# Linear attention block on one core: phi of q on pairs of PSUM banks, one normalising instruction per block of rows, and a changed order of denominators and state accumulator

## The chip, the cores and the metric

The kernel runs on one core of a Trainium2 chip. The metric is the device time of one execution in microseconds. A run is an execution with its own time and with a record of the TensorE clock that was granted, as a share of full speed. Most quoted times are medians of 4 to 11 executions on the same chip, the kernel's executions with executions of the kernel before interleaved in the same rounds. Faster or slower needs a difference of 2%; inside it, an interval of the ratio that leaves out 1 still shows a difference. An execution counts as slow, and is left out, when it takes over 1.5% longer than the fastest of the same kernel; the others are called fast. The sets of rounds ran on different chips, so a comparison between sets carries about 0.1 us of doubt. The span that the profile shows is about 1.7 us shorter than the device time.

Engines: PE is TensorE's matmul stream, PEld its weight loads, DVE is VectorE, ACT is ScalarE, POOL is GpSimd, SP the queue that issues most DMAs.

## The reference, cut to what matters

```python
B, S, D = 1, 2048, 640; H = 32; Dh = 20
q, k, v = split_heads(x @ wqkv)                       # cut: reshape and transpose
phi = lambda t: where(t > 0, t + 1, exp(t)) + 1e-6
pq, pk = phi(q), phi(k)
kv  = einsum("bhsd,bhse->bhde", pk, v)
z   = einsum("bhsd->bhd", pk)
num = einsum("bhqd,bhde->bhqe", pq, kv)
den = einsum("bhqd,bhd->bhq", pq, z)[..., None] + 1e-6
out = merge_heads(num / den) @ wo                     # cut: transpose and reshape
```

The kernel computes phi as min(exp(t), 1) + 1e-6 + max(t, 0), and 1/den as exp(-ln(den)).

## The kernel before

Its stages are: 16 k tiles (matmul, exp on ScalarE, two instructions on VectorE); two passes of state matmuls over the 16 row tiles (`p_step`), with the sum z of phi(k) on VectorE beside them (`z_steps`); the small per-head products (`kv_group`, `w2_group`), which go through HBM to change their layout (`w2_rows`, arriving as `w2p`); the q stage, 20 tiles of 128 columns by 512 rows; four denominators (`den`) and four normalisings; 16 output tiles. Every engine gets a list of instructions, in the order of the calls below; the trace after the change shows VectorE keeping to it (zc read at 64.58 us, though its input was complete at 62.89). Waits on semaphores are derived from the tiles and banks that each instruction reads and writes. The program divides PSUM, the memory that the matmuls write, into 8 banks of 512 columns; it makes a matmul into a bank wait until the bank's last reader is done.

```python
def p_step(h, st):
    def mm(e):
        for d in range(NC_):                     # 5 accumulators, banks 0 to 4
            r = e.matmul(bank(d, HALF), xn[...], pk[...], start=(st == 0), stop=(st == NT - 1))
        return r
    P.add("pe", mm, reads=[("xn", st // 4), ("pk", st)], writes=[("bank", d) for d in range(NC_)])

def q_tile(sbk, c, b):
    ...                                          # 5 matmuls of 128x512 into bank b
    P.add("act", lambda e: e.activation(t[:, :], bank(b), ACTF.Exp), ...)
    P.add("dve", lambda e: e.tensor_scalar(t[:, :], t[:, :], 1.0, 1e-6, ALU.min, ALU.add), ...)
    P.add("dve", lambda e: e.scalar_tensor_tensor(pq[...], bank(b), 0.0, t[:, :], ALU.max, ALU.add), ...)

def z_finish(b):                                 # 5 products with a single column (shown by the profile as 10 fp32 matmuls)
    ...
    P.add("dve", lambda e: e.tensor_copy(zc[:, 0:NC_], bank(b, NC_)), ...)
    for c in range(NC_):
        P.add("dve", lambda e, c=c: e.tensor_scalar(zb[...], hm[:, :], zc[:, c:c + 1], None, ALU.mult), ...)

def den(sbk, b):
    ...                                          # 5 matmuls zb x pq into bank b; needs all of zb
    P.add("act", lambda e: e.activation(lb[i][:, :], bank(b), ACTF.Ln, bias=eps[:, 0:1]), ...)
    P.add("act", lambda e: e.activation(rd[i][:, :], lb[i][:, :], ACTF.Exp, scale=-1.0), ...)

def normalize(sbk):
    for c in range(NC_):
        P.add("dve", lambda e, v=v: e.tensor_tensor(v, v, rd[i][:, :], ALU.mult), ...)

# after the state passes (cut: the calls before and after)
kv_group(0)
next_q(5)
z_finish(4)
w2_group(0, 2)
next_q(6)
w2_group(1, 0)
den(0, 4)
next_q(7)
...
```

## Time and profile before

| | |
|---|---|
| median (range) | 111.82 us (111.79 to 111.96), 4 executions, granted clock 1.00 in the profiled one |
| span of the profile | 110.1 us |
| PE busy | 101.5 us, 92% |
| DVE, ACT busy | 66.9 us, 41.9 us |

The page's second part cuts the span into 40 slices of 2.75 us; each digit is the busy share in tenths (9 is 90% or more), and PEclk is the granted clock in tenths.

```profile
PE   5969999999799999999999999993999799999990
...
PEclk9999999999999999999999999999999999999999
```

PE is close to full from the first k tile to the end, with one hole in the q stage (the 3) and a few smaller ones. The same matmuls run before and after the change (662 recorded on each of the two pages). The view of waits names the larger holes; its columns are the waiting engine and line, what it waited for, total us, times, longest us:

```profile
...
PE ps L275 <- DVE pq L288: 1.8, 1, 1.8
...
PE ps L249 <- DVE pk L240: 0.7, 1, 0.7
...
```

The second line is the first state step, which waits for bank 4 to be read by the last phi of k but one. The timeline of PE where the q stage begins (start, length of the run, line, count):

```profile
60.21 1.25 PE L275 MATMUL ps<-xT,wqp 128*128 128x512 bf16 x5
61.30 1.17 PE L325 MATMUL ps<-ones,zs 128*128 128x1 f32 x10
62.33 0.46 PE L365 MATMUL ps<-wog,kvt 120*120 120x320 bf16 x2
62.85 1.02 PE L275 MATMUL ps<-xT,wqp 128*128 128x512 bf16 x4
63.71 0.44 PE L365 MATMUL ps<-wog,kvt 120*120 120x320 bf16 x2
64.21 1.25 PE L391 MATMUL ps<-pq,zb 128*128 128x512 bf16 x5
```

Between z_finish (L325) and the first denominator (L391) stand a q tile and two w2 groups. They cover most of the time in which VectorE makes zb. (Of the q tile one matmul's record is missing.) The groups of instructions that the change replaces, with total busy us and the mean ns of one:

```profile
...
L283 ACT ACTIVATE eq<-ps 128x512 bf16<-128x512 f32 x20 | 11.9, 595 | 21.2 <-PE ps L275 20.7
...
L288 DVE SCALAR_TENSOR_TENSOR pq<-ps,eq 128x512 bf16<-128x512 f32 x20 | 13.8, 692 | 0.7
L285 DVE TENSOR_SCALAR eq<-eq 128x512 bf16<-128x512 bf16 x20 | 5.8, 290 | 12.8 <-ACT eq L283 12.6
...
L407 DVE TENSOR_TENSOR pq<-pq,rd 128x512 bf16<-128x512 bf16 x20 | 7.0, 417 | 2.0 <-ACT rd L400 2.0
```

### The profile page before, as it was taken

The numbers are of one execution on the slowest core, as the hardware profiler recorded it, in microseconds if no ns is written. First come the engines' busy times: TensorE is split into PE (matmuls) and PEld (weight loads), VectorE is DVE, ScalarE is ACT, GpSimd is POOL, SyncE is SP. The second block draws the span as 40 slices with busy tenths as digits, with TensorE's granted clock in tenths as the row PEclk, the third lists the DMA queues.
The fourth block names the chain that finished last, engine by engine and source line by source line (L and its number), as shares of the span: only waits on it lengthen the run. The fifth ranks groups of instructions, "written<-read, shape, count | busy, mean of one in ns | idle before, by whom it ended". The sixth has DMA issues, their size and how long they took to land.

```text
span 110.1 us, 1693 instructions
## 1 busy us (share of the span) xinstructions
PE 101.5 (92%) x662; PEld 64.0 (58%) x668; DVE 66.9 (61%) x132; ACT 41.9 (38%) x73; POOL 5.9 (5%) x16
## 2 busy tenths in 40 slices
PE   5969999999799999999999999993999799999990
PEld 2327777777477674676757745431446377777760
DVE  1004888998899899701137664969849837333331
ACT  3104555555500206202043379872575173333330
POOL 7100000750000000000000000000000000000000
PEclk9999999999999999999999999999999999999999
DMA  1999999999980000000000000082720032433333
GB/s 40 270 295 220 224 211 298 378 363 364 258 163 22 0 0 3 0 0 0 6 0 3 0 0 0 18 216 70 206 92 0 0 119 92 152 119 119 119 120 118
DMA packets 19497, 12.88 MB, mean 117 GB/s; under 512 B 10914, under 2 KB 19490, under 8 KB 19490
## 3 DMA queue, kind: packets, MB, share of 16 engines
q1 hardware_dynamic: 18178, 11.96, 39.4%
q10 hardware_dynamic: 1312, 0.82, 2.7%
q8 instruction: 5, 0.08, 0.3%
q14 instruction: 2, 0.02, 0.0%
HBM read 6.72 MB, written 3.44 MB: 92 GB/s over the span
## 4 chain that ended last, share of the span: by engine, by line
PE 70%; DVE 15%; DMA 6%; ACT 5%; issue 1%
PE ps L225 19%; PE ps L416 17%; PE ps L249 15%; PE ps L275 12%; DMA xT<-in_x_dram 6%; DVE pq L288 4%; PE ps L391 4%; DVE za L294 4%; ACT eq L283 2%; DVE eq L285 2%; DVE pq L407 2%; PE ps L344 1%; ACT lb L398 1%; PE ps L365 1%; ACT rd L400 1%
## 5 line engine op out<-in xcount | busy, mean ns | idle before, releaser
L275 PE MATMUL ps<-xT,wqp 128*128 128x512 bf16 x95 | 23.0, 379 | 2.0 <-DVE pq L288 1.8
L249 PE MATMUL ps<-pk,xn 128*128 128x320 bf16 x160 | 22.4, 299 | 0.8 <-DVE pk L240 0.7
L225 PE MATMUL ps<-wk,xT 128*128 128x320 bf16 x160 | 21.9, 299 | 1.1 <-DMA xT<-in_x_dram 1.1
L416 PE MATMUL ps<-w2p,pq 128*128 128x320 bf16 x160 | 22.2, 299 | 0.3 <-DVE pq L288 0.3
L249 PEld LDWEIGHTS ps<-pk,xn 128*128 128x128 bf16 x160 | 15.5, 98 | 7.9 <-DVE pk L240 1.0
L225 PEld LDWEIGHTS ps<-wk,xT 128*128 128x128 bf16 x160 | 15.6, 98 | 7.5 <-issue 1.5
L283 ACT ACTIVATE eq<-ps 128x512 bf16<-128x512 f32 x20 | 11.9, 595 | 21.2 <-PE ps L275 20.7
L416 PEld LDWEIGHTS ps<-w2p,pq 128*128 128x128 bf16 x160 | 15.6, 98 | 7.0 <-DVE pq L288 0.6
L235 ACT ACTIVATE ek<-ps 128x640 bf16<-128x640 f32 x16 | 11.3, 704 | 15.7 <-PE ps L225 15.7
L275 PEld LDWEIGHTS ps<-xT,wqp 128*128 128x128 bf16 x100 | 9.6, 98 | 12.2 <-DVE pq L288 2.2
L288 DVE SCALAR_TENSOR_TENSOR pq<-ps,eq 128x512 bf16<-128x512 f32 x20 | 13.8, 692 | 0.7
L285 DVE TENSOR_SCALAR eq<-eq 128x512 bf16<-128x512 bf16 x20 | 5.8, 290 | 12.8 <-ACT eq L283 12.6
L240 DVE SCALAR_TENSOR_TENSOR pk<-ps,ek 128x640 bf16<-128x640 f32 x16 | 13.2, 824 | 0.6
L425 DVE CAST osb<-ps 128x320 bf16<-128x320 f32 x16 | 7.7, 489 | 9.6 <-PE ps L416 9.5
L237 DVE TENSOR_SCALAR ek<-ek 128x640 bf16<-128x640 bf16 x16 | 6.1, 380 | 10.5 <-ACT ek L235 10.4
L423 ACT CAST osb<-ps 128x320 bf16<-128x320 f32 x16 | 6.8, 425 | 12.6 <-PE ps L416 12.5
L407 DVE TENSOR_TENSOR pq<-pq,rd 128x512 bf16<-128x512 bf16 x20 | 7.0, 417 | 2.0 <-ACT rd L400 2.0
L216 PE MATMUL ps<-zero 128*128 128x512 bf16 x16 | 5.2, 494 | 1.3 <-DVE eps L147 1.3
L261 ACT CAST pt<-ps 128x320 bf16<-128x320 f32 x6 | 2.2, 434 | 9.7 <-PE ps L249 9.7
L294 DVE TENSOR_TENSOR za<-pk 128x1280 f32<-128x1280 bf16 x4 | 5.7, 1483 | 0.0
L391 PE MATMUL ps<-pq,zb 128*128 128x512 bf16 x19 | 4.8, 380 | 0.4 <-DVE pq L288 0.3
L208 POOL COPY wqp<-wqn 128x640 bf16<-128x640 bf16 x5 | 3.6, 756 | 16.9 <-DMA wqn<-in_wqkv_dram 16.9
(30 smaller groups left out, 36.1 us busy)
## 6 DMA issues: line engine op xcount, KB each, us to landing
xn<-in_x_dram SPq DMA_DIRECT2D x4, 640.0 KB, 9.7
out_dram<-osb SPq DMA_DIRECT2D x16, 160.0 KB, 1.8
wk<-in_wqkv_dram ACTq DMA_DIRECT2D x2, 400.0 KB, 5.0
wqn<-in_wqkv_dram SPq DMA_DIRECT2D x1, 800.0 KB, 5.2
wv<-in_wqkv_dram SPq DMA_DIRECT2D x1, 800.0 KB, 14.3
w2p<-w_rows SPq DMA_DIRECT2D x5, 160.0 KB, 2.7
wog<-in_wo_dram SPq DMA_DIRECT2D x1, 750.0 KB, 14.8
w_rows<-w2g SPq DMA_DIRECT2D x1, 750.0 KB, 5.3
```

Of the source, the lines that this page charges most:

```text
L225: r = e.matmul(bank(b + h, HALF), xT[:, c * S + 128 * st:c * S + 128 * st + 128], wk[:, c * D + HALF * h:c * D + HALF * (h + 1)], start=(c ...
L235: P.add("act", lambda e: e.activation(fold(t[:, :]), two_banks(b), ACTF.Exp), reads=banks + ["table"], writes=[("ek", st % 3)])
L240: P.add("dve", lambda e: e.scalar_tensor_tensor(fold(pk[:, st * D:(st + 1) * D]), two_banks(b), 0.0, fold(t[:, :]), ALU.max, ALU.add), rea ...
L249: r = e.matmul(bank(d, HALF), xn[:, st * D + 128 * d:st * D + 128 * d + 128], pk[:, st * D + HALF * h:st * D + HALF * (h + 1)], start=(st ...
L275: r = e.matmul(bank(b), wqp[:, d * D + 128 * c:d * D + 128 * c + 128], xT[:, d * S + BK * sbk:d * S + BK * (sbk + 1)], start=(d == 0), sto ...
L283: P.add("act", lambda e: e.activation(t[:, :], bank(b), ACTF.Exp), reads=[("bank", b), "table"], writes=[("eq", i)])
L285: P.add("dve", lambda e: e.tensor_scalar(t[:, :], t[:, :], 1.0, 1e-6, ALU.min, ALU.add), reads=[("eq", i)], writes=[("eq", i)])
L288: P.add("dve", lambda e: e.scalar_tensor_tensor(pq[:, c * S + BK * sbk:c * S + BK * (sbk + 1)], bank(b), 0.0, t[:, :], ALU.max, ALU.add), ...
L294: P.add("dve", lambda e: e.tensor_tensor(d_ap, a, b, ALU.add), reads=ra + rb, writes=[dst])
L391: r = e.matmul(bank(b), zb[:, 128 * c:128 * c + 128], pq[:, c * S + BK * sbk:c * S + BK * (sbk + 1)], start=(c == 0), stop=(c == NC_ - 1))
L407: P.add("dve", lambda e, v=v: e.tensor_tensor(v, v, rd[i][:, :], ALU.mult), reads=[("rd", i), ("pq", sbk, c)], writes=[("pq", sbk, c)])
L416: r = e.matmul(bank(b + h, HALF), pq[:, c * S + 128 * st:c * S + 128 * st + 128], w2p[:, c * D + HALF * h:c * D + HALF * (h + 1)], start=( ...
```

## The change

Its intent is fewer and longer instructions on ScalarE and VectorE in the q stage, no wait at the first state step, and denominators whose logs do not stand in the way of the next exps. The functions, cut to the core:

```diff
-        def p_step(h, st):
+        def p_step(h, st, ds=range(5)):        # any of the five accumulators
+        def q_pair(sbk, c, b):
+            ...                                # 10 matmuls, banks b and b + 1
+            src = ps[:, BK * b:BK * (b + 2)]
+            P.add("act", lambda e: e.activation(t[:, :], src, ACTF.Exp), ...)      # 1024 columns
+            P.add("dve", ... tensor_scalar(t[:, :], t[:, :], 1.0, 1e-6, ALU.min, ALU.add), ...)
+            P.add("dve", ... scalar_tensor_tensor(pq_cols(sbk, c, c + 2), fold(src, BK), 0.0, ...), ...)
+        def den_act(sbk, b):                   # Ln and Exp of den, now called separately
         def normalize(sbk):
-            for c in range(NC_): ...
+            P.add("dve", lambda e: e.tensor_tensor(
+                v, v, rd[i][:, :].unsqueeze(1).broadcast_to([128, NC_, BK]), ALU.mult), ...)
```

The order of the calls (the rest is cut):

```diff
         for h in range(2):
             for st in range(NT):
-                p_step(h, st)
+                if h == 0 and st < 2:
+                    p_step(h, st, range(4))
+                    if st == 1:
+                        p_step(h, 0, [4])
+                        p_step(h, 1, [4])
+                else:
+                    p_step(h, st)
         kv_group(0)
-        next_q(5)
+        q_pair(1, 1, 2)
         z_finish(4)
-        w2_group(0, 2)
-        next_q(6)
-        w2_group(1, 0)
-        den(0, 4)
-        next_q(7)
+        w2_group(0, 0)
+        den(0, 5)
+        w2_group(1, 6)
+        q_pair(1, 3, 2)
+        den_act(0, 5)
         ...
-        for st in range(2):
-            out_tile(st)
-        den(3, 6)
+        out_tile(1, 2)
+        out_tile(0, 6)
+        den(3, 4)
+        den_act(3, 4)
         normalize(3)
```

Of the 14 q tiles that remain after the state passes, 12 become 6 pairs; 2 stay single.

More of the change, by code (lines that the diff above doesn't have):

```diff
@@ L110, in bass_standalone__linear_attn_block__prompt_kernel @@
         pq = sb("pq", NC_ * S)
-        eq = [sb(f"eq{j}", BK) for j in range(3)]
+        eq = [sb(f"eq{j}", 2 * BK) for j in range(3)]
         pt = sb("pt", NC_ * D)
@@ L243, in k_tile @@
                 reads=banks + [("ek", st % 3)], writes=[("pk", st)])
-        def p_step(h, st):
+        def p_step(h, st, ds=range(5)):
             def mm(e):
-                for d in range(NC_):
+                for d in ds:
                     r = e.matmul(
@@ L254, in p_step @@
             P.add("pe", mm, reads=[("xn", st // 4), ("pk", st)],
-                  writes=[("bank", d) for d in range(NC_)])
+                  writes=[("bank", d) for d in ds])
         def p_out(h):
@@ L282, in q_tile, with mm @@
             t = eq[i]
-            P.add("act", lambda e: e.activation(t[:, :], bank(b), ACTF.Exp),
+            P.add("act", lambda e: e.activation(t[:, 0:BK], bank(b), ACTF.Exp),
                   reads=[("bank", b), "table"], writes=[("eq", i)])
+            P.add("dve", lambda e: e.tensor_scalar(
+                t[:, 0:BK], t[:, 0:BK], 1.0, 1e-6, ALU.min, ALU.add),
+                reads=[("eq", i)], writes=[("eq", i)])
+            P.add("dve", lambda e: e.scalar_tensor_tensor(
+                pq[:, c * S + BK * sbk:c * S + BK * (sbk + 1)], bank(b), 0.0, t[:, 0:BK],
+                ALU.max, ALU.add),
+                reads=[("bank", b), ("eq", i)], writes=[("pq", sbk, c)])
+        def q_pair(sbk, c, b):
+            i = nq[0] % 3
+            nq[0] += 1
+            for k in range(2):
+                def mm(e, k=k):
+                    for d in range(NC_):
+                        r = e.matmul(
+                            bank(b + k),
+                            wqp[:, d * D + 128 * (c + k):d * D + 128 * (c + k) + 128],
+                            xT[:, d * S + BK * sbk:d * S + BK * (sbk + 1)],
+                            start=(d == 0), stop=(d == NC_ - 1))
+                    return r
+                P.add("pe", mm, reads=[("wqp", d) for d in range(NC_)]
+                      + xT_keys(BK * sbk, BK * (sbk + 1)), writes=[("bank", b + k)])
+            banks = [("bank", b), ("bank", b + 1)]
+            t = eq[i]
+            src = ps[:, BK * b:BK * (b + 2)]
+            P.add("act", lambda e: e.activation(t[:, :], src, ACTF.Exp),
+                  reads=banks + ["table"], writes=[("eq", i)])
             P.add("dve", lambda e: e.tensor_scalar(
@@ L288, in q_tile, with pq_cols @@
             P.add("dve", lambda e: e.scalar_tensor_tensor(
-                pq[:, c * S + BK * sbk:c * S + BK * (sbk + 1)], bank(b), 0.0, t[:, :],
+                pq_cols(sbk, c, c + 2), fold(src, BK), 0.0, fold(t[:, :], BK),
                 ALU.max, ALU.add),
-                reads=[("bank", b), ("eq", i)], writes=[("pq", sbk, c)])
+                reads=banks + [("eq", i)], writes=[("pq", sbk, c), ("pq", sbk, c + 1)])
+        def pq_cols(sbk, c0, c1):
+            return pq[:, :].rearrange("p (c s) -> p c s", s=S)[
+                :, c0:c1, BK * sbk:BK * (sbk + 1)]
         def z_add(dst, d_ap, a, b, ra, rb):
@@ L404, in normalize, with out_tile @@
             i = sbk % 2
-            for c in range(NC_):
-                v = pq[:, c * S + BK * sbk:c * S + BK * (sbk + 1)]
-                P.add("dve", lambda e, v=v: e.tensor_tensor(v, v, rd[i][:, :], ALU.mult),
-                      reads=[("rd", i), ("pq", sbk, c)], writes=[("pq", sbk, c)])
-        def out_tile(st):
-            b = 2 * (st % 4)
+            v = pq_cols(sbk, 0, NC_)
+            keys = [("pq", sbk, c) for c in range(NC_)]
+            P.add("dve", lambda e: e.tensor_tensor(
+                v, v, rd[i][:, :].unsqueeze(1).broadcast_to([128, NC_, BK]), ALU.mult),
+                reads=[("rd", i)] + keys, writes=keys)
+        def out_tile(st, b):
             j = st % 4
@@ L460, in bass_standalone__linear_attn_block__prompt_kernel @@
         kv_group(0)
-        next_q(5)
+        q_pair(1, 1, 2)
         z_finish(4)
-        w2_group(0, 2)
-        next_q(6)
-        w2_group(1, 0)
-        den(0, 4)
-        next_q(7)
-        w2_group(2, 2)
-        next_q(5)
-        w2_group(3, 0)
-        normalize(0)
-        next_q(6)
-        w2_group(4, 2)
-        next_q(7)
-        w2_group(5, 0)
-        den(1, 4)
-        w2_rows()
-        next_q(5)
-        next_q(6)
+        w2_group(0, 0)
[3 more added lines that the diff above has]
+        den_act(0, 5)
+        w2_group(2, 0)
+        w2_group(3, 6)
+        q_pair(2, 0, 4)
+        w2_group(4, 0)
+        normalize(0)
+        w2_group(5, 6)
+        w2_rows()
+        den(1, 2)
+        q_pair(2, 2, 0)
+        den_act(1, 2)
+        q_tile(2, 4, 3)
+        q_pair(3, 0, 6)
         normalize(1)
-        while qi[0] < 15:
-            next_q((7, 2, 3, 5, 6)[qi[0] % 5])
-        next_q(0)
-        next_q(1)
         den(2, 4)
-        next_q(2)
+        q_pair(3, 2, 0)
+        den_act(2, 4)
+        q_tile(3, 4, 5)
         normalize(2)
-        next_q(3)
-        next_q(5)
-        for st in range(2):
-            out_tile(st)
-        den(3, 6)
+        out_tile(1, 2)
+        out_tile(0, 6)
+        den(3, 4)
+        den_act(3, 4)
         normalize(3)
         for st in range(2, NT):
-            out_tile(st)
+            out_tile(st, 2 * (st % 4))
         block = es(nc.Block())
```

## The prediction

> **What bounds it now.** TensorE. The page's first part has PE busy 101.5 of 110.1 us, at full granted clock in every slice; VectorE (DVE) 61%. PE's matmul work is the same before and after, so only PE's idle stretches can change the time. The waits view and the timeline show these after the start: 0.66 us at 30.05 (first state step, for VectorE's last read of bank 4), about 0.3 at 44.46 (VectorE's copies of pt), about 0.3 at 64.21 (zb), 1.75 at 76.08 (q matmul, bank not yet read by VectorE), 0.3 at 86.15, 0.3 at 87.30.

> **What changes, costed.**
> 1. Fifth accumulator moved back: the 0.66 us at 30.05 goes. But VectorE's four z adds (5.69 us from 31.26) do not move. VectorE then idles 0.45 us before the first q tile at 37.40; only that can be won, since z adds, zs and pt copies (ending 44.41) hold PE's second half. Gain 0.45 to 0.5.
> 2. phi on pairs. Single-bank durations in the trace: exp 595 ns, min/add 290, max/add 692. The two-bank exp I estimate at 1.02 us, from 0.595 and the 0.85 ns per element between the 512- and 640-element exps (595, 704 ns)[...]. Min/add 0.42, max/add 1.22 (from 824 against 692 ns). A pair then takes 2.66 us from its last matmul to its last write, a tile 1.6.
> 3. Normalising: five multiplies took 1.76 us; one of 2560 elements I estimate at 1.48[...].
> 4. Order around the first denominator. On VectorE q_pair(1,1) now stands before zc and zb. Before, PE had a w2 group, a q tile and another w2 group after z_finish to hide zb. Now, after the pair (2.2 us of PE), z_finish (1.03) and one w2 group (0.28), PE meets den(0), which needs zb; zb comes after the pair's exp, min, max (2.66), zc 0.15, zb 0.90. Estimate: PE idles 2.7 us there instead of 0.25: loss 2.45.
> 5. Later in the q stage. The waits of 1.75, 0.3 and 0.3 go; small ones come: about 0.2, 0.2, 0.3 and 0.15 for banks that ScalarE frees later, 0.8 before den(2), 0.3 before den(3), 0.9 before the third output tile, whose bank 4 den(3)'s log still reads. Sum 2.9 against 2.6: loss 0.25.

> The same arithmetic on the kernel before puts PE's waits where the trace has them and its end within 0.4 us.

> **Sum:** -0.5 + 2.45 + 0.25 = +2.2 us: 114.05 us, range 113.3 to 114.9, essentially on the 2% line (114.07). Chances: faster by over 2% 0.04, within 2% 0.48, slower by over 2% 0.48.

> **What would show it.** Step 1: no PE wait at about 29.4, VectorE continuous from 31.3 to 38. Steps 2 and 3: groups of about 1.02, 0.42, 1.22 and 1.48 us. Step 4: in the waits view, den(0)'s weight load or matmul waiting about 2.7 us for zb, near 63 to 66 us. Step 5: no PE wait over 1 us after that.

> **What would make it wrong.** A pair instruction costing more than linear;[...] PE's clock falling in the 2.7 us idle; w2p landing after the first output tile wants it (about 85 us, margin under 0.3); or the later bank waits being fewer than I count, leaving the change near level.

What the trace before shows for durations: exp 595 and 704 ns for 512 and 640 elements, 0.85 ns per element, so about 1.03 us for 1024 (the text has 1.02). Min/add, for which the text gives no source: medians of 294 ns for 512 and 328 for 640, so about 0.43 us for 1024 (0.42 in the text). The five multiplies start 335 ns apart and take 417 ns each, which makes the 1.76 us; that one of 2560 elements takes 1.48 was the estimate, which these numbers do not yield; the trace after has 1.484.

## The result, and the profile after

The changed kernel took 116.60 us (116.02 to 116.94, 4 executions) against 111.82 us (111.79 to 111.96) of the kernel before. The ratio is 1.0419, with a 95% interval of 1.0368 to 1.0471. Ratios in this text are the mean time of one kernel's fast runs over that of the other's in the same rounds, so they are not quite the ratio of the medians quoted. The granted clock of the four executions was 0.983, 0.970, 0.983 and 0.970.

The page's second part after, over a span of 114.3 us:

```profile
PE   5979999999999998999999199999797979999990
...
PEclk9999999999999999999999958999999999999999
```

There is a new hole in PE (the 1), and behind it two slices in which the clock is not full. The waits of PE after:

```profile
...
PE ps L422 <- DVE zb L363: 2.7, 1, 2.7
...
PE ps L449 <- ACT lb L431: 0.8, 1, 0.8
PE ps L449 <- DMA w2p<-w_rows: 0.7, 1, 0.7
PE ps L422 <- DVE pq L288: 0.7, 1, 0.7
...
```

The wait of the q matmuls for a bank (1.8 us before) and of the first state step (0.7 us) are gone. The new wait for zb is larger than either. The timeline around it, with the instructions of PE, ACT and DVE that belong to its chain:

```profile
59.55 2.33 PE L299 MATMUL ps<-xT,wqp 128*128 128x512 bf16 x10
...
61.72 1.17 PE L356 MATMUL ps<-ones,zs 128*128 128x1 f32 x10
61.92 1.02 ACT L310 ACTIVATE eq<-ps 128x1024 bf16<-128x1024 f32 x1 [3.21 <-PE ps L299]
...
62.75 0.46 PE L396 MATMUL ps<-wog,kvt 120*120 120x320 bf16 x2
62.97 0.43 DVE L312 TENSOR_SCALAR eq<-eq 128x1024 bf16<-128x1024 bf16 x1 [2.36 <-ACT eq L310]
...
63.43 1.23 DVE L315 SCALAR_TENSOR_TENSOR pq<-ps,eq 128x1024 bf16<-128x1024 f32 x1
64.58 0.15 DVE L360 COPY zc<-ps 128x5 f32<-128x5 f32 x1
64.77 0.90 DVE L363 TENSOR_SCALAR zb<-hm,zc 128x128 bf16<-128x128 bf16 x5
...
65.95 1.80 PE L422 MATMUL ps<-pq,zb 128*128 128x512 bf16 x4 [2.74 <-DVE zb L363]
...
68.08 3.01 PE L299 MATMUL ps<-xT,wqp 128*128 128x512 bf16 x10
```

Two things are to be seen. First, z_finish's matmuls end before 63 us, but VectorE reads their result (zc) only at 64.58: its list has the pair's two instructions first, and those wait for the pair's exp. VectorE kept to the order of its list: zc's input was complete at 62.89 us, before DVE started the pair's first instruction at 62.97, and zc still came behind it. Second, after the wait the same matmuls take longer: ten of 128x512 took 2.33 us at 59.55 and 3.01 us at 68.08, and the four that are recorded of the first denominator 1.80 us. The busy times by stretch show why; the columns are the stretch, its length, busy us and count for PE, PEld, DVE, ACT and POOL, then the granted clock and DMA:

```profile
64.00:66.00 2.00, 0.05 (x1) 0.16 (x3) 1.63 (x7) 0.00 (x0) 0.00 (x0) 1.00 0.00 0
66.00:68.00 2.00, 2.00 (x6) 0.96 (x6) 0.00 (x0) 0.00 (x0) 0.00 (x0) 0.51 0.00 0
68.00:70.00 2.00, 2.00 (x8) 0.80 (x6) 0.00 (x0) 0.69 (x1) 0.00 (x0) 0.63 0.00 0
70.00:72.00 2.00, 2.00 (x13) 1.20 (x11) 0.00 (x0) 0.87 (x1) 0.00 (x0) 1.00 0.00 0
```

From the end of the wait to about 69.4 us PE ran at half clock (0.50 in 69.0:69.4, where matmuls of 128x512 start 427 ns apart; 1.00 in 69.6:70.0, and 216 ns). PE is shown busy all the while; only the count of matmuls and the PEclk column betray it.

The new instructions cost what was forecast (compare the groups shown before):

```profile
...
L310 ACT ACTIVATE eq<-ps 128x1024 bf16<-128x1024 f32 x6 | 6.2, 1026 | 10.7 <-PE ps L299 10.7
L312 DVE TENSOR_SCALAR eq<-eq 128x1024 bf16<-128x1024 bf16 x6 | 2.6, 427 | 12.9 <-ACT eq L310 12.9
...
L315 DVE SCALAR_TENSOR_TENSOR pq<-ps,eq 128x1024 bf16<-128x1024 f32 x6 | 7.3, 1225 | 0.2
L440 DVE TENSOR_TENSOR pq<-pq,rd 128x2560 bf16<-128x2560 bf16 x4 | 5.9, 1484 | 1.2 <-ACT rd L433 1.2
```

### The profile page after: what moved, and what is told of

It is laid out like the page before. It is cut to its first block, busy times and chain, and to the rows that moved or that the text cites. A ratio compares the mean times of both kernels' runs of the same rounds, so it can differ in the third digit from the quotient of the medians.

```text
span 114.3 us, 1657 instructions
## 1 busy us (share of the span) xinstructions
PE 103.6 (91%) x662; PEld 64.4 (56%) x668; DVE 64.0 (56%) x104; ACT 40.7 (36%) x67; POOL 6.0 (5%) x16
## 4 chain that ended last, share of the span: by engine, by line
PE 60%; DVE 15%; DMA 13%; ACT 7%; SPq 2%; issue 1%
PE ps L449 19%; PE ps L225 19%; PE ps L249 10%; DVE za L325 9%; DMA xT<-in_x_dram 6%; DMA w_rows<-w2g 5%; PE ps L299 4%; PE ps L275 3%; ACT eq L310 3%; PE ps L422 2%; DMA w2p<-w_rows 2%; SPq L414 2%; ACT w2g L401 2%; PE ps L375 1%; ACT lb L431 1%
## 5 line engine op out<-in xcount | busy, mean ns | idle before, releaser
L299 PE MATMUL ps<-xT,wqp 128*128 128x512 bf16 x60 | 14.8, 393 | 0.1
L237 DVE TENSOR_SCALAR ek<-ek 128x640 bf16<-128x640 bf16 x16 | 5.4, 339 | 10.8 <-ACT ek L235 10.7
L310 ACT ACTIVATE eq<-ps 128x1024 bf16<-128x1024 f32 x6 | 6.2, 1026 | 10.7 <-PE ps L299 10.7
L312 DVE TENSOR_SCALAR eq<-eq 128x1024 bf16<-128x1024 bf16 x6 | 2.6, 427 | 12.9 <-ACT eq L310 12.9
L283 ACT ACTIVATE eq<-ps 128x512 bf16<-128x512 f32 x8 | 4.7, 593 | 13.3 <-PE ps L275 13.3
L275 PE MATMUL ps<-xT,wqp 128*128 128x512 bf16 x36 | 8.9, 379 | 0.2
L422 PE MATMUL ps<-pq,zb 128*128 128x512 bf16 x18 | 5.3, 431 | 3.5 <-DVE zb L363 2.7
L315 DVE SCALAR_TENSOR_TENSOR pq<-ps,eq 128x1024 bf16<-128x1024 f32 x6 | 7.3, 1225 | 0.2
L440 DVE TENSOR_TENSOR pq<-pq,rd 128x2560 bf16<-128x2560 bf16 x4 | 5.9, 1484 | 1.2 <-ACT rd L433 1.2
```

Of the source, the lines that this page charges most:

```text
L275: r = e.matmul(bank(b), wqp[:, d * D + 128 * c:d * D + 128 * c + 128], xT[:, d * S + BK * sbk:d * S + BK * (sbk + 1)], start=(d == 0), sto ...
L299: r = e.matmul(bank(b + k), wqp[:, d * D + 128 * (c + k):d * D + 128 * (c + k) + 128], xT[:, d * S + BK * sbk:d * S + BK * (sbk + 1)], sta ...
L310: P.add("act", lambda e: e.activation(t[:, :], src, ACTF.Exp), reads=banks + ["table"], writes=[("eq", i)])
L315: P.add("dve", lambda e: e.scalar_tensor_tensor(pq_cols(sbk, c, c + 2), fold(src, BK), 0.0, fold(t[:, :], BK), ALU.max, ALU.add), reads=ba ...
L422: r = e.matmul(bank(b), zb[:, 128 * c:128 * c + 128], pq[:, c * S + BK * sbk:c * S + BK * (sbk + 1)], start=(c == 0), stop=(c == NC_ - 1))
```

## The experiments

Theory A: zb stands behind the pair's chain on VectorE, so PE waits 2.7 us; the wait makes the clock fall, and this fall is what the time has above the forecast. Rival B: the excess lies in the two-bank instructions and their bank waits in general, or the clock falls for a reason other than the wait. All kernels below gave correct results. The kernel before, in their rounds, had medians of 111.84 to 111.98 us. Executions are fast ones unless stated.

### 1. The clock alone: keep the wait, keep PE busy in it

```diff
         w2_group(0, 0)
+        fill(12)      # 12 matmuls of zeros into bank 7, which nobody reads
         den(0, 5)
```

> The changed kernel with 12 dummy matmuls of zeros (about 2.6 us at full clock) on TensorE in the place where it waits 2.74 us for zb before the first denominator. All else stays, and the wait's end (zb) does not move. Theory A (the extra over the forecast is the halved clock that follows the wait): granted clock 1.00 in every slice, matmuls 216 ns apart after the wait, 114.0 to 114.5 us, and no faster 116.0/116.9 split. Rival B (the extra lies elsewhere, in bank waits, or the clock falls for another reason than the idle): clock stays 0.97 to 0.983 and the time 116 to 117.

Measured: 114.12 us (114.00 to 114.26), ratio 1.0189 (1.0159 to 1.0219), granted clock 1.00 in all four executions. The timeline of PE:

```profile
63.54 2.54 PE L222 MATMUL ps<-zero 128*128 128x512 bf16 x11
66.00 1.25 PE L428 MATMUL ps<-pq,zb 128*128 128x512 bf16 x5
...
67.36 2.32 PE L305 MATMUL ps<-xT,wqp 128*128 128x512 bf16 x10
```

The first denominator starts no earlier (66.00 against 65.95 us): nothing useful moved. Useless work took 2.5 us off the changed kernel. So the clock's fall accounts for 2.5 us (116.60 less 114.12) and the rest of the change for 2.3 us (114.12 less the 111.85 us of its rounds). The forecast had 2.2 for that rest. The two sets of executions come from different rounds, and 2.5 us is the median over two kinds of executions of the changed kernel (1.7 and 2.7 us, experiment 9).

### 2. The wait: z_finish ahead of the first pair

```diff
-        q_pair(1, 1, 2)
         z_finish(4)
+        q_pair(1, 1, 2)
```

> The changed kernel with z_finish (and so zc and zb on VectorE) moved ahead of the first q pair. Theory A (the place of zb behind the pair's 2.66 us chain makes the wait, and the wait the clock's fall): no wait over 1.4 us, clock 1.00, and the forecast's arithmetic gives -1.4 us for the wait on top of the clock: 112.5 to 113.1 us. Rival B (two-bank instructions and their bank waits as such are the cost): 114.5 us or more.

Measured: 112.92 us (112.42 to 113.15), clock 1.00 in all four, ratio 1.0079 (1.0042 to 1.0116). The wait for zb is gone; a wait of 1.21 us for the second pair's bank (read by the first pair's last instruction) took part of its place, within the 1.4 us that the expectation allowed:

```profile
PE ps L299 <- DVE pq L315: 1.2, 1, 1.2
```

Moving one line takes 3.7 us off the changed kernel. Rival B's 114.5 us or more did not come.

### 3. Single tiles in the changed order

```diff
-        q_pair(1, 1, 2)
+        q_tile(1, 1, 2)
+        q_tile(1, 2, 3)
         # and so for the other five pairs
```

> The changed kernel in its new order, but every q pair made of two single-bank q tiles. Theory A: a single tile's chain behind the last matmul is 1.6 us instead of 2.66, so TensorE waits for zb about 1.6 us instead of 2.74, short enough for the clock to stay at 1.00, and the later bank waits shrink: 111.8 to 112.5 us. Rival B (the order alone is to blame, pairing is neutral): the wait stays near 2.7 us, 115 us or more.

Measured: 112.57, 112.64, 112.70 and 114.17 us, ratio 1.0094 (1.0027 to 1.0162). The profiled execution has a wait of 1.65 us for zb, and its clock is 1.00. The three lower times lie just over the top of the range (112.5); a wait of 0.59 us ahead of the first output tiles, which the forecast did not have, is there in its trace. The fourth execution had clock 0.985: the clock fell here too, in 1 of 4. The shorter chain of a single tile, which gives its bank back sooner, is worth almost 4 us here (116.60 less 112.67), most of it through the clock (2.5 us, experiment 1).

### 4. Single tiles, z_finish first, another bank for the last denominator

```diff
-        den(3, 4)
-        den_act(3, 4)
+        den(3, 0)          # out_tile(2) uses bank 4
+        den_act(3, 0)
         # with the edits of 2 and 3
```

> Single-bank q tiles, z_finish ahead of them, and the fourth denominator in bank 0 so that the third output tile does not wait for its log (bank 4). The accumulator's move and the one-instruction normalising stay. Theory A: TensorE has no wait over 0.5 us from 44 us on; 109.3 to 110.2 us, faster than both kernels by about 2 per cent. Rival B (order neutral or harmful): no faster than before, 111.8 us or more.

Measured: 110.48 us (110.16 to 110.72), ratio 0.9866 (0.9834 to 0.9897): faster than both kernels, but 0.3 us outside the range of theory A, and 1.3% faster than before where 2% was expected. The waits show what was left out:

```profile
PE ps L449 <- DMA w2p<-w_rows: 0.9, 1, 0.9
PE ps L249 <- DVE pt L264: 0.4, 1, 0.4
```

With nothing else in its way, PE reaches the output tiles before w2p has arrived from HBM.

### 5. What pairing costs when zb is out of the way

As 4, but with the pairs kept.

> Pairs against singles with all else equal: z_finish ahead of the first q pair and the fourth denominator in bank 0, pairs kept. Against the same with single tiles (110.48 us) this shows what pairing itself costs where zb is out of the way. Theory A (a pair holds two banks for 2.66 us and TensorE waits for them): 1.2 to 2.2 us slower than with singles, 111.7 to 112.6 us, and 0.3 to 1.0 us faster than the version with only z_finish moved (112.92). Rival B (pairing is harmless once zb is early): 110.3 to 110.9 us.

Measured: 112.19 us (112.03 to 112.23), ratio 1.0014 (0.9993 to 1.0036). Pairing costs 1.7 us against the same order with single tiles (110.48 us, in another set of rounds whose kernel before differed by 0.13 us). Both this and the 0.7 us below are in theory A's ranges. The waits behind it are mainly PE's 1.2 us for the second pair's bank and 0.7 us before the third denominator (0.2 with single tiles). The other bank for the last denominator is worth 0.7 us (112.92 less 112.19).

### 6. The accumulator's move alone, on the kernel before

```diff
+                if h == 0 and st < 2:
+                    p_step(h, st, range(4))
+                    if st == 1:
+                        p_step(h, 0, [4])
+                        p_step(h, 1, [4])
+                else:
+                    p_step(h, st)
```

> The kernel before with the accumulator's move alone (the fifth state accumulator of the first two steps issued behind the other eight matmuls). Forecast's step 1: the 0.66 us wait at 30.05 goes, but VectorE's z adds give only 0.45 to 0.5 of it on: 111.3 to 111.5 us. Rivals: all of 0.66 is won (111.1 to 111.2), or nothing (111.8).

Measured: 111.40 us (111.29 to 111.83, 6 executions), ratio 0.9956 (0.9934 to 0.9979). The mean gain is 0.4% of 112 us, so 0.5 us, as forecast. The interval, 0.2 to 0.7 us, does not by itself exclude the rival of 0.66 us. Its trace does show where a part of the gain goes: PE now waits 0.43 us for VectorE's pt copies, a wait that was 0.14 us in the timeline of the kernel before.

### 7. The one-instruction normalising alone, on the kernel before

The edit is the change's `normalize`.

> The kernel before with the one-instruction normalising alone. The forecast's durations (1.48 us for five multiplies that took 1.76) put this at 0.2 to 0.3 us faster than before, 111.5 to 111.7 us, all of it at the normalising on the chain before the output tiles. Rival: no gain that the rounds can tell (111.8 or more), as the wait moves to w2p or to the next bank.

Measured: 111.61 us (111.55 to 111.64, 5 executions), ratio 0.9977 (0.9964 to 0.9990): 0.26 us, as forecast. Both of the change's smaller parts are gains by themselves.

### 8. What makes the clock fall

In the changed kernel the wait follows z_finish, whose matmuls have one column each. If these counted as idleness (a guess, here put to the test), the light stretch would be not 2.74 but about 4.2 us (61.72 to 65.95, with 0.46 us of a w2 group's matmuls in it). To part the two, a dead add of 1.485 us delays zb on VectorE, and 7 dummy matmuls stand between z_finish and the wait:

```diff
         q_pair(1, 1, 2)
+        z_add(("za", 1), za[1][:, :], za[1][:, :], za[2][:, :], ...)    # result unused
         z_finish(4)
         w2_group(0, 0)
+        fill(7)
         den(0, 5)
```

> What makes the clock fall: a 2.7 us wait by itself, or the wait together with the light one-column matmuls of z_finish just before it. One dead 1.485 us add is put on VectorE ahead of zc, and 7 dummy matmuls of zeros (1.5 us) on TensorE behind z_finish and the w2 group: the wait stays about 2.7 us but now follows 1.5 us of dense matmuls. If the wait alone decides, the clock falls as before (about 0.98 or 0.97) and the time is 1.4 us over the changed kernel's 116.6, about 118. If the light work counts as idle too (4.05 us in all, now broken up), the clock stays near 1.00 and the time is about 115.5 us, 1.4 over the version with 12 dummy matmuls (114.12).

Measured: 115.34, 115.47, 115.62 us with clock 1.00, 0.997 and 1.00, and one slow execution, 117.34 us with clock 0.983. This looked like the branch in which the light matmuls count. But the bare wait had come out at 2.41 us, not 2.7, so a longer one was run, with 5 dummy matmuls:

> As the version with the dead add and 7 dummy matmuls, where the wait came out at 2.41 us, but with 5, so that the bare wait is about 2.8 us, no shorter than the changed kernel's 2.74, behind 1.1 us of dense matmuls. If the bare wait decides, every execution falls to 0.97 to 0.985 and takes about 117.5 us. If the light one-column matmuls in front count as idle too, most executions keep 1.00 and take about 115.5, as 3 of 4 did with 7.

Measured: 117.21 us (116.93 to 117.44), clock 0.985, 0.984, 0.984, 0.984. The bare wait of the profiled execution was 2.83 us:

```profile
67.39 1.25 PE L428 MATMUL ps<-pq,zb 128*128 128x512 bf16 x5 [2.83 <-DVE zb L369]
```

```profile
66.00:68.00 2.00, 0.61 (x3) 0.31 (x4) 1.30 (x7) 0.00 (x0) 0.00 (x0) 1.00 0.00 0
68.00:70.00 2.00, 2.00 (x8) 0.96 (x7) 0.00 (x0) 0.69 (x1) 0.00 (x0) 0.65 0.00 0
```

The wait ended at 67.39 us. The clock was full until 68 us and half for 1.4 of the next 2 us (2 x (1 - 0.65) / 0.5; the stretch 70:72 has 0.50), so by this estimate it fell at about 68.6 us, when dense matmuls had already run for 1.2 us.

### 9. The two kinds of executions of the changed kernel

> The changed kernel unaltered, for the distribution of its granted clock (4 executions so far: 0.983, 0.983, 0.970, 0.970) and, if the profiled execution falls in it, a trace of the 0.970 kind. Theory A: every execution shows the clock fallen; the 116.9 us kind has a second or a twice as long half-clock stretch behind the wait for zb. Rival B: some executions keep the clock at 1.00 and take about 114.

Measured, 6 executions: 115.28, 115.58, 116.00 us with clock 0.983 to 0.985, and 116.62, 116.79, 117.12 us with 0.970 (the last counts as slow by its distance from the fastest). Not one kept its clock. The ratio of the fast ones was 1.0385 (1.0342 to 1.0427). The profiled execution was of the first kind, so one more was taken:

> The changed kernel once more, one profiled execution, to catch the 0.970 kind (5 of 10 executions so far) in a trace. If it is caught, it shows whether the half clock lasts about 6.8 us behind the wait for zb or falls a second time at a later wait (0.7 us before the third denominator, or before the output tiles). If it is the 0.983 kind, that stays open.

Measured: one execution, 116.77 us, clock 0.970 (a single run, its state is unknown), with a trace of the second kind:

```profile
64.00:66.00 2.00, 0.00 (x0) 0.13 (x2) 1.55 (x7) 0.00 (x0) 0.00 (x0) 0.62 0.00 0
66.00:68.00 2.00, 1.96 (x5) 0.90 (x5) 0.00 (x0) 0.00 (x0) 0.00 (x0) 0.50 0.00 0
68.00:70.00 2.00, 2.00 (x7) 0.77 (x6) 0.00 (x0) 0.69 (x1) 0.00 (x0) 0.50 0.00 0
70.00:72.00 2.00, 2.00 (x8) 0.85 (x7) 0.00 (x0) 0.00 (x0) 0.00 (x0) 0.67 0.00 0
```

Here the clock fell inside the wait, at about 64.5 us, and came back at about 71.3: 6.8 us in one piece, of which some 1.5 us lie in the wait and cost nothing. The remaining 5.3 us at half clock lose 2.7 us; the mean of its four fast executions is 116.82 us, 2.70 over experiment 1. The first kind has 3.4 us at half clock, which loses 1.7 us; its five executions average 115.83 us, 1.71 over experiment 1. Both kinds are thus accounted for.

This trace also bears on the light matmuls. The timeline ahead of the fall:

```profile
61.63 1.17 PE L356 MATMUL ps<-ones,zs 128*128 128x1 f32 x10
62.66 0.46 PE L396 MATMUL ps<-wog,kvt 120*120 120x320 bf16 x2
66.04 1.91 PE L422 MATMUL ps<-pq,zb 128*128 128x512 bf16 x4 [2.92 <-DVE zb L363]
```

PE's last matmul ended at 63.12 us, so the bare wait was only 1.4 us old when the clock fell, shorter than the 1.75 us wait that the kernel before passes at full clock (1.00 in 72:74, 74:76 and 76:78). Between these two traces the length of the bare wait does not decide; in front of this one stood the one-column matmuls. That these made the difference was not shown: it is one trace, and no run was built to test it.

### 10. A version that beats both

The accumulator's move and the one-instruction normalising are kept. All q tiles are single. z_finish runs in a free bank in the middle of the second state pass, and the last z step behind the pt copies. The order of the rest was chosen by carrying each engine's list forward with the durations of the trace until PE met no wait:

```diff
-                if zst and st % 2 == 1:
+                if zst and st % 2 == 1 and st < 15:
+                if h == 1 and st == 9:
+                    z_finish(6)
         kv_group(0)
-        ...
+        den(0, 4); den_act(0, 4); normalize(0)
+        w2_group(2, 0); q_tile(1, 1, 3); w2_group(0, 6); q_tile(1, 2, 5); w2_group(1, 0)
+        q_tile(1, 4, 4); w2_group(4, 2); q_tile(1, 3, 1); w2_group(3, 6); w2_group(5, 2)
+        q_tile(2, 0, 0); q_tile(2, 2, 4); q_tile(2, 3, 1); w2_rows(); q_tile(2, 1, 2)
+        q_tile(3, 2, 7); q_tile(2, 4, 1); q_tile(3, 3, 4)
+        den(1, 6); den(2, 3); den_act(1, 6); den_act(2, 3)
+        q_tile(3, 4, 7); q_tile(3, 0, 1); q_tile(3, 1, 5); out_tile(1, 2); out_tile(0, 6)
+        normalize(1); den(3, 2); den_act(3, 2); normalize(3); normalize(2)
         for st in range(2, NT):
             out_tile(st, 2 * (st % 4))
```

> A version meant to beat both: accumulator's move and one-instruction normalising kept, all q tiles single-bank, z_finish in a free bank during the second state pass, the last z step after the pt copies, denominators, w2 groups and q tiles in an order in which TensorE finds every operand ready. Theory A (all that is to be had is TensorE's waiting): no TensorE wait over 0.3 us from 29 us on, clock 1.00, 107.6 to 108.6 us, 3 to 4 per cent faster than before. Rival B (the order moves waits rather than removes them): 109.5 us or more.

Measured: 107.85 us (107.77 to 108.05), ratio 0.9632 (0.9610 to 0.9654), so 3.7% faster than before. The page, over a span of 106.3 us:

```profile
PE   5999999999999999999999999999999999999990
...
PEclk9999999999999999999999999999999999999999
```

PE's only listed wait is the one of 1.3 us at the very start. What was to be had in the q stage was PE's waiting, and most of it came from order and banks, not from cheaper instructions.

## Why the prediction was right or wrong

It forecast +2.2 us (114.05 us, 113.3 to 114.9) and +4.8 us came. The direction and the largest term that it priced were right; a term of the same size was missing, and the time lay outside the range.

- **What bounds it (right).** PE; only its idle time or its clock could change the time.
- **Step 1, the accumulator (right).** Forecast 0.45 to 0.5 us; alone it gave 0.5 us. After the change PE's first state step starts at 29.10 us without a wait, and VectorE runs on from the z adds to the first q tile.
- **Step 2, durations of the pair's instructions (right).** Forecast 1.02, 0.42 and 1.22 us; measured 1.026, 0.427 and 1.225. For the exp that is 0.84 ns for each element from 512 (595 ns) to 1024, beside 0.85 from 512 to 640.
- **Step 3, normalising (right).** Forecast 1.48 us, measured 1.484, where the five single multiplies took 1.76. Alone it gave 0.26 us.
- **Step 4, the wait for zb (right in place and size, wrong in its worth).** Forecast 2.7 us, measured 2.74. The prediction priced the wait at its length, "loss 2.45". It cost that and then 1.7 or 2.7 us more, as the matmuls behind it ran at half clock for 3.4 or 5.3 us.
- **Step 5, later waits (the large ones right, the sum in part by luck).** Forecast 0.8 before the third denominator and 0.9 before the third output tile; measured 0.66 and 0.78. The 0.3 before the fourth denominator did not come, and of the four small bank waits, 0.15 to 0.3 each, the trace of experiment 1 shows two, of 0.07 and 0.11 us. In their place came a wait for w2p, named only as a risk: 0.2, 0.4 and 0.7 us in the three traces of the changed kernel, 0.33 us in experiment 1.
- **The step that failed** is the sum itself: "-0.5 + 2.45 + 0.25 = +2.2 us" has no term for the clock. "PE's clock falling in the 2.7 us idle" stood among the things that would make it wrong, and it is what did; it should have been priced. Why it was left out is not on record. A possible reason: the kernel before has a wait of 1.75 us and keeps its clock (1.00). The term measured 2.5 us on the medians (1.7 or 2.7 by the kind of execution). Without it the forecast is within 0.1 us: experiment 1 took 114.12 us. So close a match is in part luck, by what step 5 had missed on either side.

The change's main idea, q tiles in pairs, worked against it (the one-instruction normalising did not, experiment 7). The change saved busy time on two engines that were not the limit (the page's first part: DVE 66.9 to 64.0 us, ACT 41.9 to 40.7) and made the delay from a tile's last matmul to the free bank longer on the engine that is (the three instructions take 2.68 us for a pair and 1.58 us for a single tile, by the means of their groups).

## What to carry to other kernels

In this kernel, where TensorE is the limit, merging instructions of another engine was worth only what it took off the waits of TensorE's (0.26 us for the normalising), and it lengthened others (1.7 us for the pairs): ask how long a bank stays occupied and what else stands behind the longer instruction in that engine's list. A small result that TensorE will need (here zb) belongs ahead of the large work on its engine, as early as its input exists (one line moved took 3.7 us off the changed kernel). Price a TensorE wait that comes near the lengths at which the clock fell here (2.74 us, or 2.92 in one trace, in all 11 executions; 2.83 us in 4 of 4; 2.41 us, or 1.65 us behind one-column matmuls, in 1 of 4 each; every length is that of a profiled execution) at more than its length: look at the granted clock and at the count of matmuls per stretch behind it, and, if such a wait can't be moved, know that dummy matmuls in it saved 2.5 us here. The kernel before, with 1.75 us in its profiled execution, kept its clock: the lowest of its 30 executions in the experiments is 0.997.
